# Gram blocks masked over all 128 rows, and a join's correction as one masked addition

## The chip, the core and the metric

One core of a Trainium2 chip runs the whole program. The metric is device microseconds of one execution, from the first instruction to the last.

## What is computed

The program chains three things. First a delta-rule recurrence over 768 tokens for 4 batches and 8 heads of 48 columns, then a gated product, then a soft mixture of experts:

```python
k_n = k / (norm(k) + 1e-6)
for t in range(S):                       # per batch and head, state is 48 x 48
    y[t]  = q[t] @ state
    v_old = state.T @ k_n[t]
    state = state + beta[t] * outer(k_n[t], v[t] - v_old)
x = (x @ w1) * (x @ w2) @ w3 @ w_out     # 3072 tokens, 384 -> 1024 -> 1024 -> 384
logits = x @ phi                         # 32 slots
dispatch = softmax(logits, over tokens); combine = softmax(logits, over slots)
out = combine @ experts(dispatch.T @ x)
```

Inputs arrive in float32 and, for some weights, float64.

## The kernel before, in words

The recurrence runs in 24 steps of 32 tokens. For each step the 32 x 32 Gram blocks of the keys (one for each batch and head) are multiplied on TensorE (PE), masked to their lower triangle by VectorE (DVE), and the inverse of a unit lower triangular matrix is formed from them. Four steps make a solve: 128 blocks, one to a lane. Steps are taken in pairs, and a pair's keys and queries lie in one tile of seven "slots" of 512 columns. Rows 64 to 112 hold batches 0 and 1 (slots 3 to 6), rows 0 to 48 batches 2 and 3 (slots 3 to 0): in the lower half the order of what is needed runs downwards. So in the products' result (tile `gp`, `g` or `p`) the Gram block is the first block of a head for two batches and the last one for the other two, and the scores and the products across the two steps also lie at different places in the two halves of the rows.

`g_step` issues those products (L420), `g_evac` brings them out of PSUM: the Gram blocks by one masked multiplication for rows 0 to 63 and one for rows 64 to 127 (L369, into tile `dg`); the scores through a copy on ScalarE (ACT, L380) and a masked multiplication on GpSimd (POOL) or DVE (L389, L396); the products across steps by ACT (L402). A PSUM bank is given to the next user when all of these have read it.

The first two solves use halves: `sub16` inverts the two 16 x 16 diagonal blocks on DVE, `join` puts them together and turns them (L523, L525), and `join2(n4)`, one for each of the four steps, forms the block below the diagonal by two sets of 32 x 2 small products on PE (L534, then L541 from the tile `xn`, 16 columns a block) with a copy on ACT between them (L538). Its result, 16 rows in each of the four groups of 32 rows, is subtracted from `w` by four DVE operations of 16 rows (L545). The later four solves take all 32 rows at once on DVE (L501, L504).

Beside the recurrence run the conversions of the float64 weights (L284 to L301 for the gates' weights, tiles `t_w`, `gx`, `raw_w`; then tile `hold` for w_out and w3, with products on PE, L316 to L350, that yield the logits' weights `wphi`), and the gated products of each pair of steps, "a chunk" (L687, tile `ab`, 144 matmuls in eight groups a chunk, 12 chunks). Steps are listed with a time each; a scheduler turns the list into one order per engine, and each engine runs its own order strictly, waiting at semaphores. The tile `ab` and the Gram products of steps 4 to 7 share two PSUM banks.

Of the kernel before, what the change touches and what calls it, by code (L numbers as in the profile page):

```python
# [21 lines left out]
C = 32  # tokens of one step of the recurrence  # L22
NST = S // C
NCH = NST // 2  # two steps: 256 rows of the products that follow
NSS = NST // 4  # four steps: 128 blocks of 32 x 32, one to a lane
NE = 8

# columns of the constant block
# [8 lines left out]
C_N = 418  # L37
# [56 lines left out]
def make_consts():  # L94
    c = np.zeros((128, C_N), np.float32)
    p = np.arange(128)
    i = np.arange(32)
    c[:, C_ID:C_ID + 128] = np.eye(128)
    c[p, C_ID4 + p % 32] = 1.0
    c[:, C_REP:C_REP + 128] = (p[:, None] % 32) == (p[None, :] % 32)  # L100
    c[:, C_ML:C_ML + 32] = i[None, :] <= (p[:, None] % 32)
    # a row's own batch's columns, of two; from C_MA on the other's
    for h in range(3):
        c[:, C_MU + 32 * h:C_MU + 32 * h + 32] = (i[None, :] > (p[:, None] % 32)) & ((p[:, None] // 32) % 2 == h % 2)
    c[:, C_QM] = (p // 32) % 2 == 0
    c[:, C_EB] = -(896.0 + 20.0) * 2.0**23
    return c


def diag(ap):  # L110
    """of each row of NE groups of 36, the first 4 of each: expert e's columns among its 32 from 32e on"""
    return ap[:, :, :].rearrange("p f (e s) -> p f e s", s=36)[:, :, :, 0:4]
# [3 lines left out]
def kern(ctx, tc, kq, vt, kt, bl, w12, w3, wo, phi, w1e, w2e, consts, out):  # L116
# [38 lines left out]
    ecT = pc.tile([128, NSS, 128], F32, name="ecT")  # L155
    u4 = pc.tile([128, 512], F32, name="u4")
# [3 lines left out]
    # two of four copies, for high and for low parts  # L160
# [5 lines left out]
    # the gates' weights, high and low parts, a column block of both in one tile  # L166
    wsl = [pv.tile([128, 2, 2, 3, 128], F32R, name=f"wsl{f}") for f in range(8)]
    # v of a step (rows of its batch) and the state (the other half's rows), batch by batch
    sv = px.tile([128, 4, H * D], F32, name="sv")
    sacc = [ps.tile([128, 512], F32, name=f"sacc{i}") for i in range(2)]  # L170
    # two steps at a time; keys and queries by column of their products: what is multiplied with the state in the rows of
    # the state, the scores in the others. Of the slots 3 has the first step's keys of all batches; 4 its queries, 5 and 6
    # the second step's keys and queries of the first two batches; 2, 1 and 0 likewise of the last two.
    kls = [pw.tile([128, 7, 512], F32, name=f"kl{i}") for i in range(3)]

    # the other weights' conversion takes turns in it, then the converted w_out comes back to it
# [4 lines left out]
    def warm(n, after):  # L181
        """keeps the array's clock up while it waits for what follows"""
# [4 lines left out]
    # once those weights are converted, pairs of steps take turns in it too  # L187
    held4 = hold[:, 0:7 * 512].rearrange("p (k c) -> p k c", k=7)

    def kl_of(p):  # L190
        """where the keys and queries of a pair of steps are"""
# [3 lines left out]
    def before(p):  # L195
        """the pair of steps that was there before"""
# [8 lines left out]
    def when(t, *steps, label="when"):  # L205
        """steps at time t, in the order given"""
# [13 lines left out]
    def srow(b):  # L220
        """rows of the state of batch b"""
# [5 lines left out]
    def trow(n, b):  # L227
        """rows of the tokens of a step: the first step of two has the batches of a pair the other way round"""
# [47 lines left out]
    def to_f32(r, n, name):  # L276
# [6 lines left out]
        # sign * 2^(e - 20)  # L283
# [3 lines left out]
        # the mantissa, 2^20 .. 2^21  # L287
# [38 lines left out]
    def w3_steps():  # L326
        part = {}

        def cv(f, j0):
            """row block f, column blocks j0 .."""  # L330
# [25 lines left out]
    Dg = {}  # L356

    def own(r, c):
        """of a half's columns those of batch c of the two"""
        return r.rearrange("p (h c i) -> p h c i", h=H, c=2)[:, :, c]  # L360

    def g_evac(n, hs, gp, at_, via):
        """gp: row, head, block, column; at_: which block the Gram block, the scores and the two across steps are"""
        s, n4 = divmod(n, 4)
        t, nh = kl_of(n // 2), len(hs)
        if "g" in at_:
            for i in range(2):
                r = slice(64 * i, 64 * i + 64)
                V.tensor_tensor(out=Dg[s][r, 8 * n4 + hs[0]:8 * n4 + hs[0] + nh, :], in0=gp[r, :, at_["g"][i], :],  # L369
                                in1=cs[r, C_ML:C_ML + 32].unsqueeze(1).to_broadcast([64, nh, 32]), op=ALU.mult)  # L370
# [3 lines left out]
        src = [gp[64 * i:64 * i + 64, :, at_["p"][i], :] for i in range(2)]  # L374
# [8 lines left out]
        for i in range(2):  # L383
            r = slice(64 * i, 64 * i + 64)
            if n % 2 == 0:
                # each batch's in its own columns, zeros in the other's
# [5 lines left out]
            for c in range(2):  # L392
# [6 lines left out]
                else:  # L399
                    x = at_["x"][i]  # L400
                    to = t[ro, (5, 0)[i]:(5, 0)[i] + 2, cols].rearrange("p k (h c i) -> p k h c i", h=nh, c=2)
                    A.copy(to[:, :, :, 1 - c], gp[ro, :, x:x + 2, :].rearrange("p h k i -> p k h i"))  # L402

    def g_step(n, hs, which="gp"):
        """of a step's keys with the keys and queries of it and, from the first of two steps, of the second"""
# [5 lines left out]
        # first and last slot of each half's  # L411
# [5 lines left out]
        for h in hs:  # L417
            for b in range(4):
                r, kc, j = srow(b), kcol(h, b), b // 2
                T.matmul(gp[trow(n, b), h - hs[0]], lhsT=t[r, k[j], kc], rhs=t[r, span[j][0]:span[j][1], kc],  # L420
                         start=True, stop=True)
        blocks = {}
        if "g" in which:
            blocks["g"] = (0, nb - 1)
        if "p" in which:
            o = len(which) - 1
            blocks["p"] = (o, nb - 1 - o)
            blocks["x"] = (o + 1, 0)
        g_evac(n, hs, gp, blocks, n < PP)

    def g_parts(p):
        """of two steps"""
# [7 lines left out]
    def solve_steps(s):  # L440
# [4 lines left out]
        def a():  # L445
# [8 lines left out]
            # 1/sqrt: a first guess from the exponent, then Newton steps  # L454
# [30 lines left out]
            if halves:  # L485
                st["tmp"] = sm[:, 5:9].rearrange("p a b -> p (a b)")
                st["xf"] = pk.tile([128, 32, 32], F32, tag="L", name=f"xf{s}", bufs=NL)
                xn = (u4[:, :], ecT[:, 0:4, :].rearrange("p s c -> p (s c)"))[s]
                st["xn"] = xn.rearrange("p (u c) -> p u c", c=16)
# [4 lines left out]
        def sub(j):  # L494
            # two column ranges in turn: neither waits for its own result
# [11 lines left out]
        def sub16(j):  # L507
            # the two diagonal blocks in turn
# [8 lines left out]
        def join():  # L517
            """the block below the diagonal ones: minus the product of the lower one, the Gram block and the upper one"""
# [8 lines left out]
        def join2(n4):  # L527
# [11 lines left out]
            for u in range(8):  # L539
                for b in range(4):  # L540
                    T.matmul(p2[32 * b:32 * b + 16, u], lhsT=xn[qrow(b), 8 * n4 + u, :], rhs=t1[qrow(b), u, :],  # L541
                             start=True, stop=True, tile_position=(32 * b, 32 * b))
            for b in range(4):
                r = slice(32 * b, 32 * b + 16)
                V.tensor_tensor(out=w[r, us, 16:32], in0=w[r, us, 16:32], in1=p2[r], op=ALU.subtract)  # L545
# [14 lines left out]
    xT = {}  # L560

    def copy(n, b, o, i):
        """two engines at the start, when nothing hides the recurrence"""
# [5 lines left out]
    def chain_steps(n):  # L569
# [13 lines left out]
        def ks():  # L583
            # the second step takes the first's part along
# [59 lines left out]
    def join_max():  # L644
        """running maxima of the token streams joined; how much of each stream's sums is left"""
# [19 lines left out]
    ecs, early_g = {}, []  # L665

    def main_steps(c):
# [56 lines left out]
        def soft():  # L724
# [29 lines left out]
            # weights of the slots for each token  # L754
# [13 lines left out]
        def uu():  # L768
# [12 lines left out]
            else:  # L781
                # the last ones with what is left of each stream
# [27 lines left out]
    def behind0(f):  # L810
        """VectorE's part of f after the first inverses"""
# [5 lines left out]
    def behind_w12(f, k):  # L817
        """VectorE's part of f after that of the k-th conversion"""
# [5 lines left out]
    def close_att():  # L824
        """the attention's memory goes to the first weights that follow"""
# [440 lines left out]
```

## Time and profile before

| | before |
|---|---|
| runs | 664.26 us median of 3 (664.17 to 665.92) |
| span of the profiled execution | 663.6 us |
| PE busy | 566.2 us, 85% |
| DVE busy | 425.8 us, 64% |
| ACT busy | 279.8 us, 42% |
| POOL busy | 160.6 us, 24% |
| mean granted clock of TensorE | 0.882 of full speed |

PE is the busiest engine over the whole span, but not in every stage. The first 41 us are keys, Gram blocks and the first solve; up to about 215 us weights are converted; up to about 612 us the recurrence and the gated products fill PE; the rest is the experts. A stage's limit is read from its own rows: the table of windows tells which engine is nearly always busy, the chain of waits tells what was last.

### The profile page before, as it was taken

What the parts mean: (1) busy time and instruction counts of PE and PEld (TensorE: products, weight loads), DVE (VectorE), ACT (ScalarE), POOL (GpSimd) and SP (SyncE); (2) the same over time, 40 slices, a digit from 0 to 9 for tenths busy, and PEclk for the clock granted to TensorE, in tenths of its full rate; (3) what the DMA queues carried; (4) which work ended last, traced back from release to release, by engine and by line L of the source; (5) the groups of instructions that cost most, each with busy time, mean ns of one, the idle gap of its engine ahead of it and who ended that gap; (6) DMA issues with size and microseconds to landing.
All of it is one profiled execution on the core that took longest, in us unless ns stands there. A gap on an engine that the chain in (4) does not pass through costs nothing.

```text
span 663.6 us, 26054 instructions
## 1 busy us (share of the span) xinstructions
PE 566.2 (85%) x11417; PEld 470.5 (71%) x11417; DVE 425.8 (64%) x1315; ACT 279.8 (42%) x704; POOL 160.6 (24%) x213
## 2 busy tenths in 40 slices
PE   5345635888999799899988998998999999999996
PEld 4234534786778677677878886887878899885464
DVE  4997899999887136984379833997993313133214
ACT  1516552435555256444444354444434444333113
POOL 1725865423452026122030101103110000000100
PEclk7555658877979799899999897999999999999997
DMA  9903503448653720400404013030445040678848
GB/s 199 321 9 126 166 0 124 146 122 214 211 158 116 171 67 17 124 2 15 106 4 93 2 34 86 15 82 14 117 125 183 31 147 3 240 253 283 338 182 277
DMA packets 36945, 81.72 MB, mean 123 GB/s; under 512 B 4352, under 2 KB 17792, under 8 KB 35584
## 3 DMA queue, kind: packets, MB, share of 16 engines
q1 hardware_dynamic: 36832, 80.07, 40.1%
q8 instruction: 89, 1.46, 0.9%
q14 instruction: 24, 0.20, 0.1%
HBM read 69.57 MB, written 10.49 MB: 121 GB/s over the span
## 4 chain that ended last, share of the span: by engine, by line
PE 48%; DVE 35%; issue 5%; DMA 5%; POOL 3%; ACT 2%; SPq 0%; DVEq 0%; POOLq 0%; ACTq 0%
PE ab L687 22%; DVE tmp L501 4%; DVE xl L504 4%; PE gp L704 2%; PE gp L420 2%; PE yp L612 2%; DMA kl<-kq 2%; PE ks L591 2%; PE sacc L1111 2%; DVE dg L369 2%; PE hp L1090 2%; DVE xl L481 2%; PE vp L602 2%; PE sacc L622 2%; DVE gl L448 1%
## 5 line engine op out<-in xcount | busy, mean ns | idle before, releaser
L687 PE MATMUL ab<-xT,wsl 128*128 128x256 f32 x1728 | 258.3, 302 | 8.5 <-issue 3.3
L687 PEld LDWEIGHTS ab<-xT,wsl 128*128 128x128 f32 x1728 | 229.3, 202 | 23.3 <-issue 10.0
L696 DVE TENSOR_TENSOR gT<-ab,bs 128x256 f32<-128x256 f32 x84 | 35.0, 419 | 93.6 <-ACT bs L691 78.0
L691 ACT COPY bs<-ab 128x256 f32<-128x256 f32 x96 | 35.7, 372 | 83.3 <-PE ab L687 82.0
L577 POOL TENSOR_TENSOR v<-v,nnT 128x384 f32<-128x384 f32 x24 | 21.6, 900 | 137.0 <-DMA v<-vt 52.1
L504 DVE TENSOR_TENSOR xl<-xl,tmp 128x84 f32<-128x84 f32 (+35 forms) x220 | 50.2, 259 | 0.8
L567 ACT COPY sv<-vp 32x384 f32<-32x384 f32 x96 | 45.1, 470 | 13.1 <-PE vp L602 11.2
L501 DVE TENSOR_TENSOR tmp<-xl 128x84 f32<-128x84 f32 (+35 forms) x220 | 49.8, 259 | 0.6
L420 PE MATMUL gp<-kl 48*32 48x64 f32 (+1 forms) x1024 | 37.8, 280 | 13.0 <-ACT kl L402 8.7
L293 POOL TENSOR_TENSOR hold<-hold 128x384 f32<-128x384 f32 (+1 forms) x32 | 34.2, 1070 | 54.6 <-DVE hold L290 19.3
L420 PEld LDWEIGHTS gp<-kl 48*32 48x32 f32 x1024 | 26.8, 122 | 19.2 <-ACT kl L402 8.8
L705 ACT COPY gtok<-gp 128x512 f32<-128x512 f32 x48 | 28.1, 587 | 18.8 <-PE gp L704 14.9
L612 PE MATMUL yp<-sv,kl 112*32 112x48 f32 (+2 forms) x1280 | 28.4, 220 | 3.8 <-ACT sv L567 3.8
L389 POOL TENSOR_TENSOR kl<-praw,cs 64x256 f32<-64x256 f32 x28 | 22.6, 808 | 36.0 <-ACT praw L380 34.6
L402 ACT COPY kl<-gp 32x256 f32<-32x256 f32 x64 | 23.2, 363 | 19.2 <-DVE kl L389 13.1
L612 PEld LDWEIGHTS yp<-sv,kl 112*32 112x32 f32 (+2 forms) x1280 | 21.9, 118 | 10.0 <-POOL kl L389 4.1
L704 PE MATMUL gp<-cs,gT 128*128 128x128 f32 x168 | 27.5, 281 | 1.5 <-DVE xT L638 1.3
L602 PE MATMUL vp<-v,w 32*32 32x48 f32 x1536 | 26.1, 211 | 2.1 <-DVE w L552 1.4
L602 PEld LDWEIGHTS vp<-v,w 32*32 32x32 f32 x1536 | 21.1, 110 | 8.6 <-issue 3.5
L369 DVE TENSOR_TENSOR dg<-gp,cs 64x128 f32<-64x128 f32 (+1 forms) x60 | 19.8, 330 | 11.4 <-PE gp L420 10.6
L285 ACT ACTIVATE hold<-hold,cs 128x384 int32<-128x384 int32 (+1 forms) x32 | 18.7, 589 | 19.6 <-DVE hold L284 19.1
L396 POOL TENSOR_TENSOR kl<-praw,cs 32x256 f32<-32x256 f32 x28 | 23.4, 835 | 13.7 <-ACT praw L380 12.1
(250 smaller groups left out, 997.9 us busy)
## 6 DMA issues: line engine op xcount, KB each, us to landing
hold<-w SPq DMA_DIRECT2D x16, 384.0 KB, 3.7
v<-vt SPq DMA_DIRECT2D x24, 192.0 KB, 3.0
kk<-kt SPq DMA_DIRECT2D x12, 384.0 KB, 6.6
unitg<-w1e SPq DMA_DIRECT2D x6, 768.0 KB, 5.3
kl<-kq SPq DMA_DIRECT2D x8, 512.0 KB, 7.1
kl<-kq SPq DMA_DIRECT2D x8, 384.0 KB, 5.0
gx<-w SPq DMA_DIRECT2D x4, 768.0 KB, 8.1
raw_w<-w SPq DMA_DIRECT2D x4, 768.0 KB, 8.8
```

Source lines behind the costliest of these rows:

```text
L293: G.tensor_tensor(out=w, in0=m, in1=w, op=ALU.mult)
L369: V.tensor_tensor(out=Dg[s][r, 8 * n4 + hs[0]:8 * n4 + hs[0] + nh, :], in0=gp[r, :, at_["g"][i], :], in1=cs[r, C_ML:C_ML + 32].unsqueeze(1 ...
L420: T.matmul(gp[trow(n, b), h - hs[0]], lhsT=t[r, k[j], kc], rhs=t[r, span[j][0]:span[j][1], kc], start=True, stop=True)
L501: V.tensor_tensor(out=tmp[:, 0:n, lo:hi], in0=x[:, j + 1:32, j:j + 1].to_broadcast([128, n, hi - lo]), in1=x[:, j:j + 1, lo:hi].to_broadca ...
L504: V.tensor_tensor(out=x[:, j + 1:32, lo:hi], in0=x[:, j + 1:32, lo:hi], in1=tmp[:, 0:n, lo:hi], op=ALU.add)
L567: A.copy(o, i)
L602: T.matmul(p[o, h * D:(h + 1) * D], lhsT=w[o, 8 * n4 + h, :], rhs=r[o, h, :], start=True, stop=True, tile_position=(o.start, o.start))
L612: T.matmul(p[qrow(b), h * D:(h + 1) * D], lhsT=kl[r, (6, 0)[b // 2] if t2 else (4, 2)[b // 2], kcol(h, b)], rhs=sv[r, b, h * D:(h + 1) * D ...
L687: T.matmul(o, lhsT=w[:, m, k], rhs=x[:, k], start=(n == 0), stop=(n == 8))
L691: A.copy(bs, p[:, 256:512])
L696: V.tensor_tensor(out=gt, in0=p[:, 0:256], in1=bs, op=ALU.mult)
L704: T.transpose(p[:, t * 256 + i * 128:t * 256 + (i + 1) * 128], gt[:, t * 128:(t + 1) * 128], ident)
```

## The change

In the products of the half with batches 2 and 3 the slots are read backwards (a step of -1 over the slots in the moving operand). The blocks of all four batches then lie in the same order: the Gram block first, then the scores, then the products across steps. The Gram mask becomes one DVE operation over 128 rows instead of two over 64; ACT's copy of the two products across steps reads the lower half's two blocks in reverse. In a join the second product takes 32 columns of `xn` at a time (16 of the block, 16 of the next one) and so writes all 32 rows of a group; a constant column that is -1 in the first 16 rows of each 32 and 0 in the others multiplies the result, and one operation over 128 rows adds it to `w`. For the last block's 16 columns beyond the end, `u4` and `ecT` become parts of one tile `sums`, and GpSimd clears 16 columns behind each `xn`. Comments are dropped, which the diff here leaves out; lines below L420 lie 4 further on.

```diff
+C_LO = 418
-C_N = 418
+C_N = 419
+    c[:, C_LO] = -1.0 * (p % 32 < 16)

-    ecT = pc.tile([128, NSS, 128], F32, name="ecT")
-    u4 = pc.tile([128, 512], F32, name="u4")
+    sums = pc.tile([128, 512 + NSS * 128], F32, name="sums")
+    u4, ecT = sums[:, 0:512], sums[:, 512:512 + NSS * 128].rearrange("p (s c) -> p s c", c=128)

         if "g" in at_:
-            for i in range(2):
-                r = slice(64 * i, 64 * i + 64)
-                V.tensor_tensor(out=Dg[s][r, 8 * n4 + hs[0]:8 * n4 + hs[0] + nh, :], in0=gp[r, :, at_["g"][i], :],
-                                in1=cs[r, C_ML:C_ML + 32].unsqueeze(1).to_broadcast([64, nh, 32]), op=ALU.mult)
+            V.tensor_tensor(out=Dg[s][:, 8 * n4 + hs[0]:8 * n4 + hs[0] + nh, :], in0=gp[:, :, at_["g"], :],
+                            in1=cs[:, C_ML:C_ML + 32].unsqueeze(1).to_broadcast([128, nh, 32]), op=ALU.mult)
...
-                    A.copy(to[:, :, :, 1 - c], gp[ro, :, x:x + 2, :].rearrange("p h k i -> p k h i"))
+                    src_x = gp[ro, :, x:x + 2, :] if i == 0 else gp[ro, :, x + 1:x - 1:-1, :]
+                    A.copy(to[:, :, :, 1 - c], src_x.rearrange("p h k i -> p k h i"))
...
-                T.matmul(gp[trow(n, b), h - hs[0]], lhsT=t[r, k[j], kc], rhs=t[r, span[j][0]:span[j][1], kc],
-                         start=True, stop=True)
+                lo, hi = span[j]
+                slots = slice(lo, hi) if j == 0 else slice(hi - 1, lo - 1 if lo else None, -1)
+                T.matmul(gp[trow(n, b), h - hs[0]], lhsT=t[r, k[j], kc], rhs=t[r, slots, kc], start=True, stop=True)
...
-                xn = (u4[:, :], ecT[:, 0:4, :].rearrange("p s c -> p (s c)"))[s]
-                st["xn"] = xn.rearrange("p (u c) -> p u c", c=16)
+                st["xnf"] = xn = (sums[:, 0:528], sums[:, 544:1072])[s]
+                if s < 2:
+                    G.memset(xn[:, 512:528], 0.0)
+                st["xn"] = xn[:, 0:512].rearrange("p (u c) -> p u c", c=16)
...
-                    T.matmul(p2[32 * b:32 * b + 16, u], lhsT=xn[qrow(b), 8 * n4 + u, :], rhs=t1[qrow(b), u, :],
-                             start=True, stop=True, tile_position=(32 * b, 32 * b))
-            for b in range(4):
-                r = slice(32 * b, 32 * b + 16)
-                V.tensor_tensor(out=w[r, us, 16:32], in0=w[r, us, 16:32], in1=p2[r], op=ALU.subtract)
+                    T.matmul(p2[qrow(b), u], lhsT=st["xnf"][qrow(b), 16 * (8 * n4 + u):16 * (8 * n4 + u) + 32],
+                             rhs=t1[qrow(b), u, :], start=True, stop=True, tile_position=(32 * b, 32 * b))
+            V.scalar_tensor_tensor(out=w[:, us, 16:32], in0=p2, scalar=cs[:, C_LO:C_LO + 1], in1=w[:, us, 16:32],
+                                   op0=ALU.mult, op1=ALU.add)
```

The scheduler also orders what is around these operations anew. On DVE, between the last gates' weights (`t_w7`) and the first conversions in `hold`, the masks of steps 6 and 7 (`gp6`, `gp7`, into `dg1`) stood like this before:

```order
L369 TENSOR_TENSOR dg1_953<-gp6_0_1131,cs_90 64x128 x2
L286 SCALAR_TENSOR_TENSOR t_w7_751<-gx_72,t_w7_751 128x768
L288 TENSOR_SCALAR gx_72<-gx_72 128x768
L369 TENSOR_TENSOR dg1_953<-gp6_4_1159,cs_90 64x128 x2
L290 SCALAR_TENSOR_TENSOR gx_72<-gx_72 128x768
L284 TENSOR_SCALAR hold_115<-hold_115 128x384 x4
L286 SCALAR_TENSOR_TENSOR hold_115<-hold_115 128x384 x2
L288 TENSOR_SCALAR hold_115<-hold_115 128x384
L286 SCALAR_TENSOR_TENSOR hold_115<-hold_115 128x384
L288 TENSOR_SCALAR hold_115<-hold_115 128x384
L369 TENSOR_TENSOR dg1_953<-gp7_0_1187,cs_90 64x256 x2
```

and stand like this in the changed kernel (its L286, L288, L290, L292 are the L284, L286, L288, L290 of before):

```order
L288 SCALAR_TENSOR_TENSOR t_w7_744<-gx_72,t_w7_744 128x768
L642 TENSOR_TENSOR xT0_1_862<-xp1_1110,xT0_0_861 128x3x128
L290 TENSOR_SCALAR gx_72<-gx_72 128x768
L292 SCALAR_TENSOR_TENSOR gx_72<-gx_72 128x768
L286 TENSOR_SCALAR hold_114<-hold_114 128x384 x4
L288 SCALAR_TENSOR_TENSOR hold_114<-hold_114 128x384 x2
L290 TENSOR_SCALAR hold_114<-hold_114 128x384
L369 TENSOR_TENSOR dg1_943<-gp6_0_1118,cs_90 128x128
L288 SCALAR_TENSOR_TENSOR hold_114<-hold_114 128x384
L290 TENSOR_SCALAR hold_114<-hold_114 128x384
L292 SCALAR_TENSOR_TENSOR hold_114<-hold_114 128x384
```

The first mask of step 6 moved behind ten conversion operations and one other; the second one moved behind fourteen conversion operations, that of step 7 (after the rows shown) behind eight.

On PE, where step 7's products and the first gated products (`ab0_0`) begin, before:

```order
L420 MATMUL gp6_0_1131<-kl0_112 32x128 x14
L420 MATMUL gp6_4_1159<-kl0_112 32x128 x14
L534 MATMUL j00_2_1440<-w0_559,dg0_147 32x16 x7
L420 MATMUL gp7_0_1187<-kl0_112 32x64 x32
L687 MATMUL ab0_0_1342<-xT0_0_871,wsl0_101 128x256
L687 MATMUL ab0_0_1342<-xT0_1_872,wsl0_101 128x256
```

and in the changed kernel (L318 is the L316 of before, a turn of converted w_out):

```order
L424 MATMUL gp6_0_1118<-kl0_111 32x128 x14
L424 MATMUL gp6_4_1145<-kl0_111 32x128 x14
L538 MATMUL j00_2_1425<-w0_555,dg0_146 32x16 x7
L424 MATMUL gp7_0_1172<-kl0_111 32x64 x32
L318 MATMUL wot0_1316<-cs_90,hold_114 128x128 x3
L691 MATMUL ab0_0_1327<-xT0_0_861,wsl0_100 128x256
L691 MATMUL ab0_0_1327<-xT0_1_862,wsl0_100 128x256
```

The turn of the first converted w_out block now stands ahead of the first gated product. At the end of the conversions, the last product for `wphi` (L350, tile `w3tw376`) stood behind 272 gated products (L687) in PE's order and stands behind 241 now.

## Rows read from the trace of the kernel before

**Rows 1.** The page: busy time, share of the span and instructions of each engine
```profile
PE 566.2 (85%) x11417; PEld 470.5 (71%) x11417; DVE 425.8 (64%) x1315; ACT 279.8 (42%) x704; POOL 160.6 (24%) x213
```

**Rows 2.** Windows: stretch, its length, busy of PE, PEld, DVE, ACT, POOL; clock, DMA
```profile
41.00:105.00 64.00, 35.69 (x989) 30.22 (x990) 55.38 (x73) 33.29 (x68) 38.16 (x27) 0.55 0.26 78
105.00:160.00 55.00, 45.07 (x899) 39.12 (x900) 52.22 (x163) 22.09 (x50) 21.54 (x20) 0.76 0.52 156
160.00:215.00 55.00, 51.54 (x980) 41.89 (x968) 46.61 (x111) 29.42 (x74) 25.59 (x27) 0.94 0.59 172
...
400.00:500.00 100.00, 91.76 (x1941) 78.99 (x1940) 83.96 (x326) 40.12 (x103) 16.79 (x41) 0.97 0.27 72
```

**Rows 3.** Chain that ended last, 0 to 41 us: start, us, what
```profile
14.48 0.41 DVE dg L369
...
14.91 0.44 DVE dg L369
```

**Rows 4.** The same chain, 37 to 215 us: masks, a join's subtractions, a conversion on POOL
```profile
46.61 0.28 DVE w L545
...
49.14 1.85 POOL t_w L293
...
74.07 0.33 DVE dg L369
74.41 0.43 DVE dg L369
...
200.72 0.29 DVE w L545
```

**Rows 5.** Groups by form: line engine op, tiles, shapes xcount | busy us, mean ns | idle before
```profile
L420 PE MATMUL gp<-kl 48*32 48x128 f32 x512 | 25.9, 318 | 4.3 <-DMA kl<-kq 3.8 <-issue 0.5
...
L369 DVE TENSOR_TENSOR dg<-gp,cs 64x128 f32<-64x128 f32 x40 | 11.5, 287 | 9.6 <-PE gp L420 8.9
...
L534 PE MATMUL j<-w,dg 32*32 32x16 f32 x512 | 9.8, 200 | 13.4 <-DVE w L525 10.6 <-DVE w L545 2.9
L545 DVE TENSOR_TENSOR w<-w,j 16x128 f32<-16x128 f32 x32 | 9.8, 305 | 1.4 <-PE j L541 0.9
...
L534 PEld LDWEIGHTS j<-w,dg 32*32 32x32 f32 x512 | 8.1, 131 | 16.8 <-DVE w L525 10.7 <-issue 6.1
...
L541 PE MATMUL j<-t,u 32*16 32x16 f32 x256 | 3.0, 182 | 4.0 <-ACT t L538 4.0
...
L541 PEld LDWEIGHTS j<-t,u 32*16 32x16 f32 x256 | 2.5, 96 | 5.1 <-ACT t L538 4.6 <-issue 0.6
```

**Rows 6.** Timeline of DVE, 44 to 103 us: start, length (of a run: all), operation
```profile
44.38 0.55 DVE L288 TENSOR_SCALAR gx<-gx 128x768 int32<-128x768 int32 x1
44.85 0.56 DVE L288 TENSOR_SCALAR raw_w<-raw_w 128x768 int32<-128x768 int32 x1
...
89.99 0.58 DVE L369 TENSOR_TENSOR dg<-gp,cs 64x128 f32<-64x128 f32 x2
...
94.20 0.59 DVE L369 TENSOR_TENSOR dg<-gp,cs 64x128 f32<-64x128 f32 x2
94.82 0.96 DVE L290 SCALAR_TENSOR_TENSOR gx<-gx 128x768 f32<-128x768 uint32 x1
95.70 4.44 DVE L284 TENSOR_SCALAR hold<-hold 128x384 int32<-128x384 int32 x4
```

**Rows 7.** Timeline of PE, 93 to 107 us; in brackets the idle time before and its releaser
```profile
93.83 1.93 PE L420 MATMUL gp<-kl 48*32 48x64 f32 x64 [8.73 <-ACT kl L402]
...
96.99 3.98 PE L687 MATMUL ab<-xT,wsl 128*128 128x256 f32 x18 [1.23 <-ACT kl L402]
...
103.89 2.88 PE L687 MATMUL ab<-xT,wsl 128*128 128x256 f32 x12 [2.93 <-ACT praw L380]
```

**Rows 8.** What PE waited for, 400 to 500 us: us in total, times, longest
```profile
PE gp L420 <- DMA kl<-kq: 3.8, 3, 1.7
...
PE vp L602 <- DVE w L552: 1.4, 1, 1.4
```

More of the change, by code (lines that the diff above doesn't have):

```diff
@@ L373, in g_evac @@
         cols = slice(64 * hs[0], 64 * hs[0] + 64 * nh)
-        src = [gp[64 * i:64 * i + 64, :, at_["p"][i], :] for i in range(2)]
+        src = [gp[64 * i:64 * i + 64, :, at_["p"], :] for i in range(2)]
         E = V
@@ L399, in g_evac @@
                 else:
-                    x = at_["x"][i]
+                    x = at_["x"]
                     to = t[ro, (5, 0)[i]:(5, 0)[i] + 2, cols].rearrange("p k (h c i) -> p k h c i", h=nh, c=2)
-                    A.copy(to[:, :, :, 1 - c], gp[ro, :, x:x + 2, :].rearrange("p h k i -> p k h i"))
+                    src_x = gp[ro, :, x:x + 2, :] if i == 0 else gp[ro, :, x + 1:x - 1:-1, :]
+                    A.copy(to[:, :, :, 1 - c], src_x.rearrange("p h k i -> p k h i"))
     def g_step(n, hs, which="gp"):
@@ L419, in g_step @@
                 r, kc, j = srow(b), kcol(h, b), b // 2
-                T.matmul(gp[trow(n, b), h - hs[0]], lhsT=t[r, k[j], kc], rhs=t[r, span[j][0]:span[j][1], kc],
-                         start=True, stop=True)
+                lo, hi = span[j]
+                slots = slice(lo, hi) if j == 0 else slice(hi - 1, lo - 1 if lo else None, -1)
+                T.matmul(gp[trow(n, b), h - hs[0]], lhsT=t[r, k[j], kc], rhs=t[r, slots, kc], start=True, stop=True)
         blocks = {}
         if "g" in which:
-            blocks["g"] = (0, nb - 1)
+            blocks["g"] = 0
         if "p" in which:
-            o = len(which) - 1
-            blocks["p"] = (o, nb - 1 - o)
-            blocks["x"] = (o + 1, 0)
+            blocks["p"] = o = len(which) - 1
+            blocks["x"] = o + 1
         g_evac(n, hs, gp, blocks, n < PP)
```

## The prediction

> **What bounds the kernel now.** I read the busy times first. PE works 85% of the span and DVE 64% [rows 1], and by that line alone a change that only relieves DVE would be worth nothing. So I went on to the windows, stage by stage [rows 2]. From 41 to 105 us DVE is busy 55.4 of 64.0 us and PE 35.7; from 105 to 160 us DVE 52.2 of 55.0 and PE 45.1. There DVE is the limit: PE stands still 28.3 + 9.9 = 38.2 us in these two stages, most of it behind conversions. From 160 to 215 us both are near full (PE 51.5, DVE 46.6 of 55.0), and later PE is the limit (91.8 of 100.0 between 400 and 500 us), although DVE has 84.0 of work there. Third came the chain that ended last. It shows whether the operations touched here were ever what the end waited for: they were. The last two of the eight opening masks stand in it [rows 3], and so do ten subtractions of joins and nine masks between 41 and 215 us, of which the first and the last subtraction and the pair at 74 us are shown [rows 4]. POOL has a part in this chain as well: a conversion's 1.85 us on it [rows 4], so in the first stage not all is DVE.
>
> **What is removed from DVE.** A mask's time follows its elements per row: 287 ns for 64 rows of 128 elements, 305 ns for a subtraction with 16 rows of 128 elements [rows 5]. A quarter of the rows made nothing cheaper, so I take 128 rows at the price of 64, and the masked addition, with 128 elements a row again, at 0.30 us. It reads one operand more than a subtraction; its ends are 0.27 (no dearer than the shortest pieces) and 0.60 us (twice a subtraction), which would be 8 x 0.30 = 2.4 us back.
>
> Counted on the chain: of the opening pair one operation goes, 0.44 us [rows 3]. Of the masks from 41 to 215 us one of each pair goes; the pair at 74 us gives 0.43 [rows 4], that at 94 us 0.30, at 102 us 0.43 (a 256-element mask like the one at 74 us), at 180 us 0.29, at 183 us 0.34, together 1.8. Of the four subtractions of a join three go: the chain has three at 46, 113 and 126 us and one at 200 us, ten by 0.29 [rows 4], 2.9 us. The sum is 0.4 + 1.8 + 2.9 = **5.1 us**. The ends are 0 (what is not DVE in the chain takes over) and all that DVE saves before 215 us whether on the chain or not, nine mask pairs (six by 0.29, three by 0.43), six joins by 0.87, and the opening 0.44, 8.7 us.
>
> A second, smaller gain follows from the order on DVE. Two ordinary operations overlap: the one at 44.38 us lasts 0.55 and the next begins at 44.85, 0.08 us before its end. Behind a pair of masks this is not so: the pair from 94.20 us lasts 0.59, and the next operation begins at 94.82, 0.03 us after its end [rows 6]. With one start row for all, the follower may overlap again: 0.11 us for each of the ten runs counted above, 1.1 us, or nothing where the follower waits anyway. I take 0.5.
>
> After 215 us the chain still holds twelve masks' pairs, one of each worth 0.29 to 0.44 us, 4.4 us in all by the sizes above. But PE is nearly always busy there, and of its waits between 400 and 500 us only one, 1.4 us for a solve's end on DVE, is behind this work, while the longest is for a load of keys [rows 8]. I take 0.4 us, with ends 0 and 4.4.
>
> **What is added.** The second product of a join loads 32 columns of weights where it loaded 16. The first product, which has 32 columns already, keeps PE 9.8 us for 512 records, the second 3.0 us for 256 [rows 5]: 1.2 against 0.75 us a join, so at most 8 x 0.47 = 3.8 us. Later joins lie beside other work of PE; only the first has nothing but the recurrence's start behind it. I take 0.5, ends 0 and 3.8. The weight loads themselves took 96 ns with 16 columns and 131 ns with 32 [rows 5]. The Trainium skill (TensorE: Matmul & The Clock Gate, section on LDWEIGHTS, loading the stationary operand) says that a load's time goes with the number of columns alone, so it would double; the trace shows 1.4 times. By the skill's rule the eight joins' loads would go from 2 x 2.5 to 10.0 us, and all of it on the path would eat the gain.
>
> GpSimd's two clears of 16 columns and the longer row of constants I cost at nothing: GpSimd is idle three quarters of the span [rows 1] and they stand at the start, before it has scores to mask. Were that cover gone, two of its shortest operations would be late by themselves. The merged tile brings no new wait that I can find in the order; the operations on it wait for the same engines as before.
>
> **What is moved.** The masks of steps 6 and 7 stand later in DVE's order. Who waits for them is on PE: step 7's products began at 93.83 us after 8.73 us behind ACT's copies, the first gated products at 96.99 us, the next at 103.89 us after 2.93 behind ACT's copy of the scores [rows 7], and these copies come behind the masks at 89.99 and 94.20 us [rows 6]. The first mask now has the four conversions of 4.44 us [rows 6] and six others ahead of it, the second six more. With the time saved before it (about 2.5 us), I put the first gated products some 7 us later. Those at 96.99 us are 3.98 us of PE's work [rows 7], done in a gap before and now to be done later; PE has 9.9 us of idleness in the next stage [rows 2] in which they fit, if DVE lets it. I charge a third, 1.3 us, ends 0 and 4.0.
>
> **The sum.** -5.1 - 0.5 - 0.4 + 0.5 + 1.3 = -4.2 us. The profiled execution's span is 663.6 us, the median of the runs 664.3; what lies around the span is 0.7 us and doesn't change. From the span 659.4, from the median **660.1 us**.
>
> **Rivals.** *The gain is handed to PE and ends there.* At the end of the conversions PE's order has 241 gated products behind it instead of 272 (the change's section). One costs 258.3 us of busy time by 1728 in the trace, 0.15 us, so PE has 31 x 0.15 = 4.6 us more left to do at that moment. If the conversions end earlier by the 5.1 us and PE is the limit from there on, the end moves by 0.5 us: 663.8 us, no change. For it speaks PE's 51.5 of 55.0 us from 160 to 215 us [rows 2]; against it, that what PE has not done before could fill the 9.9 us in which it stood before 160 us.
>
> *Slower, by the late masks.* If the gated products' lag is not made up between 105 and 160 us, because PE's order has turns of converted weights in between that still wait for DVE and POOL, PE carries 4.0 us over into the stages where it is full, against some 1 us of gain left there: 667.3 us. It decides from the point where more than the sum's other terms, 5.5 us, would be lost, or where the conversions do not end earlier: then the lag alone remains.
>
> *Slower, by reading backwards.* No product of the trace steps backwards. The Gram products with 128 columns keep PE 25.9 us [rows 5], half of them with the backward step now. If that made them half as dear again, 13.0 x 0.5 = 6.5 us would come on a full PE: 664.3 - 4.2 + 6.5 = 666.6 us. From a third (4.2 of 13.0) on it eats the gain. Nothing in the trace speaks for it: the moving operand was already read as separate pieces of 32 columns.
>
> *It does not do what it says.* The order has 34 masks for 68 and 8 additions for 32, so DVE's operations go; only a far dearer masked addition could undo it (2.4 us above), and that leaves the result between the first two cases.
>
> **How the numbers follow.** About 0.3%, 2.0 us, is what a measurement of this kernel can tell from no change: faster is below 662.3, slower above 666.3 us. My forecast, DVE's time reaching the end less the lag, has 0.53; its own range is 656.5 to 662.3. No change, PE's share, 0.26. Slower by the late masks 0.16, by backward reading 0.05. So 0.53, 0.26 and 0.21. The lower end is all of DVE's saving before 215 us, 664.3 - 8.7 = 655.6, the upper end the late masks' 667.3 us.
>
> **What the changed profile would show.** DVE's busy time should fall by 34 masks and 24 subtractions: 20 x 0.29 + 14 x 0.43 + 24 x 0.30 = 19 us, from 425.8 to about 407 us [rows 1]. Masks should stay at 287 ns and the additions at 0.27 to 0.33 us. The first solve should begin 0.4 us earlier. Between 41 and 160 us DVE should remain above 85% busy with the conversions ending some 5 us earlier; PE's idleness before 215 us should shrink by about 4 us, or, in the first rival, stay. The first gated products should begin near 104 us. The Gram products' mean, 318 ns for 128 columns [rows 5], should not move. I would be wrong if the conversions are led by POOL or ACT, if the masked addition costs far more than a subtraction, or if the new order opens a gap on PE somewhere that neither order nor chain of before shows.

## The result, and the profile after

The changed kernel takes **657.64 us** (median of 4 runs, 655.6 to 659.15) against 665.09 us (664.17 to 666.9) for the kernel before beside it: a ratio of 0.9875, interval 0.9832 to 0.9919. In a second comparison (below) the ratio was 0.9902, interval 0.9871 to 0.9933. So it is faster by 6.5 to 8.3 us, where 4.2 us were forecast. The page of the changed kernel, and its windows as in [rows 2]:

```profile
PE 565.9 (86%) x11417; PEld 470.4 (72%) x11417; DVE 406.8 (62%) x1257; ACT 279.3 (42%) x704; POOL 167.7 (26%) x215
```

```profile
41.00:105.00 64.00, 35.53 (x992) 30.38 (x990) 54.77 (x67) 33.94 (x69) 44.49 (x29) 0.81 0.32 96
105.00:160.00 55.00, 44.42 (x874) 37.92 (x872) 50.76 (x162) 21.91 (x49) 24.41 (x22) 0.84 0.51 155
160.00:215.00 55.00, 52.60 (x927) 41.56 (x929) 39.67 (x91) 27.98 (x70) 22.14 (x23) 0.85 0.59 176
...
400.00:500.00 100.00, 95.16 (x2041) 81.67 (x2040) 80.31 (x322) 42.80 (x110) 17.73 (x42) 0.98 0.25 71
```

DVE lost 19.0 us of busy time [rows 1], the 19 us that were forecast. PE did no less. From 41 to 215 us it is busy as before: 132.55 of 174.00 us, where [rows 2] adds up to 132.30. Only later is it busier, 95.16 against 91.76 us between 400 and 500 us. (The first clock figure can't be set against [rows 2]: this profile has no clock record in its first 77 us, and the view shows 1.00 there. A second profile of the same kernel shows 0.56 in the first window.)

The groups that answer to [rows 5]: the products with 128 columns, then masks, both products of a join with their weight loads, and the masked addition.

```profile
L424 PE MATMUL gp<-kl 48*32 48x128 f32 x512 | 25.3, 317 | 5.3 <-DMA kl<-kq 4.7 <-ACT kl L404 0.7
...
L369 DVE TENSOR_TENSOR dg<-gp,cs 128x128 f32<-128x128 f32 x20 | 5.7, 286 | 15.3 <-PE gp L424 15.0
L369 DVE TENSOR_TENSOR dg<-gp,cs 128x256 f32<-128x256 f32 x10 | 4.1, 412 | 1.0 <-PE gp L424 1.0
...
L538 PE MATMUL j<-w,dg 32*32 32x16 f32 x512 | 8.7, 198 | 12.1 <-DVE w L529 12.1
L546 PE MATMUL j<-t,sums 32*32 32x16 f32 x512 | 7.7, 192 | 5.5 <-ACT t L542 5.5
...
L546 PEld LDWEIGHTS j<-t,sums 32*32 32x32 f32 x512 | 6.5, 122 | 8.0 <-ACT t L542 6.1 <-issue 1.5 <-ACT bs L695 0.2
...
L548 DVE SCALAR_TENSOR_TENSOR w<-j,cs,w 128x128 f32<-128x128 f32 x8 | 2.7, 339 | 4.5 <-PE j L546 4.5
```

A mask over 128 rows costs what one over 64 rows did (286 against 287 ns), the masked addition 339 ns where 300 were taken, and the products with 128 columns, half of them read backwards now, 317 against 318 ns on the mean. But an operation's length isn't what the next one pays. DVE's timeline (start, length, operation) of the changed kernel:

```profile
45.75 0.95 DVE L292 SCALAR_TENSOR_TENSOR raw_w<-raw_w 128x768 f32<-128x768 uint32 x1
46.62 0.35 DVE L548 SCALAR_TENSOR_TENSOR w<-j,cs,w 128x128 f32<-128x128 f32 x1
46.88 0.28 DVE L369 TENSOR_TENSOR dg<-gp,cs 128x128 f32<-128x128 f32 x1
...
94.46 0.28 DVE L369 TENSOR_TENSOR dg<-gp,cs 128x128 f32<-128x128 f32 x1
94.66 0.54 DVE L288 SCALAR_TENSOR_TENSOR hold<-hold 128x384 int32<-128x384 int32 x1
```

and of the kernel before, at its first join:

```profile
46.30 1.23 DVE L545 TENSOR_TENSOR w<-w,j 16x128 f32<-16x128 f32 x4
47.57 1.50 DVE L290 SCALAR_TENSOR_TENSOR raw_w<-raw_w 128x768 f32<-128x768 uint32 x1
```

Both new operations overlap what stands behind them here. From its start to the next start a mask takes 0.20 us (94.46 to 94.66) where a pair took 0.62 (94.20 to 94.82, [rows 6]); a join's addition takes 0.26 us (46.62 to 46.88) where four subtractions took 1.27 (46.30 to 47.57). Where the next operation waits for something else there is nothing to overlap: in this profile the next operation starts before the end of 24 of the 34 masks and of five of the eight additions.

On PE the late masks of steps 6 and 7 show as foreseen, at half the size: step 7's products and the first gated ones, as in [rows 7].

```profile
96.88 1.93 PE L424 MATMUL gp<-kl 48*32 48x64 f32 x64 [8.45 <-ACT kl L404]
99.88 0.90 PE L318 MATMUL wot<-cs,hold 128*128 128x128 f32 x3 [1.07 <-POOL hold L295]
100.43 4.76 PE L691 MATMUL ab<-xT,wsl 128*128 128x256 f32 x23
```

The gated products begin 3.4 us later than in [rows 7], where 7 us were forecast. DVE's conversions of `hold` begin at 88.92 us, 6.8 us earlier than in [rows 6], and the last of them ends at 205.29 us, where it ended at 211.76 us before.

### The profile page after: what moved, and what is told of

Same layout as the page of the kernel before. It is cut to its first block, busy times and chain, and to the rows that moved or that the text cites. A ratio compares the mean times of both kernels' runs of the same rounds, so it can differ in the third digit from the quotient of the medians.

```text
span 657.4 us, 25995 instructions
## 1 busy us (share of the span) xinstructions
PE 565.9 (86%) x11417; PEld 470.4 (72%) x11417; DVE 406.8 (62%) x1257; ACT 279.3 (42%) x704; POOL 167.7 (26%) x215
## 4 chain that ended last, share of the span: by engine, by line
PE 56%; DVE 26%; DMA 6%; issue 5%; POOL 3%; ACT 2%; SPq 0%; DVEq 0%; POOLq 0%; ACTq 0%
PE ab L691 25%; PE gp L424 3%; DMA kl<-kq 3%; DVE tmp L505 3%; PE gp L708 3%; DVE xl L508 2%; PE yp L616 2%; PE ks L595 2%; PE sacc L626 2%; PE sacc L1115 2%; PE vp L606 2%; PE hp L1094 2%; DVE hold L286 2%; PE lp L715 2%; DVE xl L483 1%
## 5 line engine op out<-in xcount | busy, mean ns | idle before, releaser
L295 POOL TENSOR_TENSOR hold<-hold 128x384 f32<-128x384 f32 (+1 forms) x32 | 36.7, 1153 | 50.1 <-DVE hold L292 12.9
L389 POOL TENSOR_TENSOR kl<-praw,cs 64x256 f32<-64x256 f32 x28 | 25.0, 894 | 37.3 <-ACT praw L380 36.0
L287 ACT ACTIVATE hold<-hold,cs 128x384 int32<-128x384 int32 (+1 forms) x32 | 18.7, 590 | 26.8 <-DVE hold L286 26.4
L626 PE MATMUL sacc<-sv,kk 64*48 64x48 f32 x704 | 26.4, 220 | 0.3 <-issue 0.3
```

The costliest lines, as they stand in the source:

```text
L295: G.tensor_tensor(out=w, in0=m, in1=w, op=ALU.mult)
L626: T.matmul(sacc[b % 2][srow(b), h * D:(h + 1) * D], lhsT=k[r, b % 2, h, :], rhs=sv[r, b, h * D:(h + 1) * D], start=False, stop=(c == NCH - 2),
```

## The experiments

Twelve kernels were run, in three sets of four, each set against the kernel before on one chip in five rounds. A difference from the kernel before goes by the ratio (1% is 6.65 us; the intervals reach 1.6 to 3.5 us to either side), one between two kernels of the same set by their medians where nothing else is said.

**The masks alone, the join alone, and the two halves without their saving on DVE.** The first takes the backward reading and the one mask, with the old join; the second only the join.

```diff
 e1_masks_only:  slots read backwards; one mask over 128 rows; four subtractions as before
 e2_join_only:   masks as before; 32 columns in the second product; one masked addition
```

> The slots are read backwards and the Gram masks are one operation over 128 rows; the joins stay as before (16-column second product, four subtractions). The masks of steps 6 and 7 stand where they stood before, ahead of the conversions. Theory 1 (the time that DVE saves before the weights are converted reaches the end): a pair of masks that took 0.62 us from its start to the next operation's start now takes 0.20, so 0.44 + 6 x 0.42 + 3 x 0.55 = 4.6 of the 10.6 us of DVE time that the whole change saves before 215 us; at the whole change's ratio (7.4 us of 10.6) -3.2 us. Theory 2 (the gain is the new order, conversions ahead of the masks of steps 6 and 7): -1 to 0 us. Theory 3 (backward reading costs something, hidden so far): DVE's saving less that cost.

Measured: 658.85 us, ratio 0.9932 (0.9909 to 0.9956), 4.5 us faster.

> Forward reading and two masks of 64 rows as before; the joins as in the change (32-column second product, one masked addition). The scheduler puts the masks of step 6 behind seven to ten conversion operations more, as in the change. Theory 1: six joins before 215 us save 1.0 us each on DVE, 6.0 of 10.6 us, so -4.2 us. Theory 2: nearly the whole, -6 to -7.4 us.

Measured: 662.21 us, ratio 0.9960 (0.9927 to 0.9992), 2.7 us faster. Both parts gain, and together they make up the 6.5 to 8.3 us. Theory 2, by which the masks alone would bring 1 us at most and the join's order the rest, fits neither. Theory 1's 3.2 and 4.2 us lie within the two intervals.

The other two kernels keep what each part puts on PE and give DVE all its operations back:

```diff
 e3_back_two_masks (slots read backwards)
+                V.tensor_tensor(out=Dg[s][r, ...], in0=gp[r, :, at_["g"], :], ...)   # r: two halves of 64 rows
 e4_wide_product (32 columns in the second product)
+            for b in range(4):
+                V.tensor_tensor(out=w[r, us, 16:32], in0=w[r, us, 16:32], in1=p2[r], op=ALU.subtract)
```

> Backward reading, with two masks of 64 rows and the joins as before; the order of DVE and PE is that of before. Theories 1 and 2: 0 us, within 0.3%. Theory 3: slower by what the backward step costs; a Gram product with 128 columns would take more than 318 ns on the mean.

Measured: 666.53 us, ratio 1.0030 (0.9997 to 1.0062): not told from no change.

> The second product of a join with 32 columns and the merged tile, but four subtractions of 16 rows as before, two masks and forward reading. The masks of step 6 stand behind the conversions as in the change, and DVE saves nothing. Theory 1: +0.5 to +2 us (0.3 us more in each second product, the masks late). Theory 2: the order alone gives most of the gain, -4 to -6 us.

Measured: 667.10 us, ratio 1.0035 (1.0008 to 1.0062), 2.3 us slower (0.5 to 4.1). Theory 2 falls: the order without DVE's saving gains nothing. The masks stand late in this kernel as in the changed one (its first gated product begins at 100.55 us), so the 2.3 us are the price of the wide product and of the late masks together. The two groups that matter, of the kernel with backward reading and of the one with the wide product:

```profile
L424 PE MATMUL gp<-kl 48*32 48x128 f32 x512 | 26.2, 320 | 5.8 <-DMA kl<-kq 4.0 <-issue 1.7
```

```profile
L545 PE MATMUL j<-t,sums 32*32 32x16 f32 x512 | 7.5, 193 | 5.3 <-ACT t L542 5.3
```

With half of them read backwards the products take 320 ns on the mean where 318 were taken before; half as much again for the backward ones would have made it 398. So the gain is DVE's: one mask for two is worth the difference of the first kernel and the third, 1.0030 - 0.9932 = 1.0%, 6.5 us; one addition for four that of the second and the fourth, 1.0035 - 0.9960 = 0.75%, 5.0 us. With the two runs' intervals taken together, either figure is good to some 2.8 us.

**Four kernels next to the changed one.** The second comparison of the changed kernel itself:

> The changed kernel itself again, on the chip and in the rounds of the three that follow, so that they can be set against it. Both theories: as measured, 657.6 us against 665.1, a ratio of 0.9875.

Measured: 659.71 us, 0.9902 (0.9871 to 0.9933).

```diff
 h2_early_masks
-G2 = -0.03
+G2 = -0.08
```

> The changed kernel with one number of the table of times moved (G2 from -0.03 to -0.08), so that the masks of steps 6 and 7 stand earlier in DVE's order again: 35, 40 and 51 conversions' operations are ahead of the three instead of 43, 49 and 53 (33, 35 and 45 before the change), and 265 gated products instead of 241 ahead of the last converted w_phi. Theory 1 (DVE's saving gives the gain, and the late masks give some of it back: 1.3 us in the forecast, up to the 2.3 us that the wide second product and the order cost together): 1.3 to 2.3 us less than the changed kernel, a ratio to the kernel before of 0.984 to 0.9855, and a first gated product some 3 us earlier than its 100.4 us. Theory 3 (the late masks cost nothing, since the gated products fit in later gaps; the wide second product is what costs): the changed kernel's time within 0.3%, a ratio of 0.986 to 0.989. Theory 2 (the new order is itself a part of the gain): 1 to 3 us more than the changed kernel, 0.989 to 0.992.

Measured: 660.39 us, 0.9936 (0.9907 to 0.9966). This kernel alters its computation: the products of steps 6 and 7 stand ahead of the load of their keys and queries, and take what lay in that memory. The load now waits 15.6 us for these products, which is a new wait, and is issued at 93.06 us where the changed kernel has it at 75.41 us. So the run doesn't price the late masks, and the forecast's 1.3 us for them stays untested by themselves.

```diff
 h3_one_score_copy
-            for i in range(2):
-                A.copy(raw[64 * i:64 * i + 64], src[i])
+            A.copy(raw, gp[:, :, at_["p"], :])
```

> The changed kernel with ACT's two 64-row copies of a pair's scores made one 128-row copy as well, which the new order of the columns allows: 24 copies fewer on ACT, 16 x 0.26 + 8 x 0.37 = 7 us of its 279. ACT's mean busy share is 42%, and these copies follow the masks. If such a copy's second half is what POOL's products of keys and scores wait for (36.0 us of POOL's idleness ends with these copies), up to 0.3 us for each of the 12 pairs before 215 us, 3 us, comes back: a ratio of 0.983. If POOL and ACT have room, as their shares say: the changed kernel's time, 0.986 to 0.989. I lean to the second.

Measured: 657.76 us, 0.9897 (0.9845 to 0.9948), the changed kernel's ratio. 24 operations fewer on ACT, which is 43% busy, bring nothing that can be told; with this interval a gain of some 3 us isn't excluded either.

```diff
 h4_late_pairs
-            V.tensor_tensor(out=Dg[s][:, ...], in0=gp[:, :, at_["g"], :], ...)
+            for r in (slice(0, 128),) if s < 2 else (slice(0, 64), slice(64, 128)):
+                V.tensor_tensor(out=Dg[s][r, ...], in0=gp[r, :, at_["g"], :], ...)
```

> The changed kernel with the masks of steps 8 to 31 in two operations of 64 rows again, and one of 128 rows for steps 0 to 7 alone: 24 operations more on DVE, 16 x 0.29 + 8 x 0.42 = 8 us of its time, nearly all after 180 us, where PE has the least idleness. The forecast put the masks after 215 us at 0.4 us with ends 0 and 4.4, and two pairs at 180 us at 0.6. Theory 1 (the gain comes from the stages in which DVE is the limit, before 180 us): 0.4 to 1.0 us more than the changed kernel, a ratio of 0.988 to 0.989. Theory 4 (DVE's time counts later too, since step follows step through its masks and joins): 3 to 5 us more, 0.992 to 0.995.

(The kernel has 24 steps, so these are steps 8 to 23.) Measured: 664.03 us, 0.9980 (0.9945 to 1.0015), **4.3 us more** than the changed kernel beside it, which leads the kernel before by 5.7 us in the same medians. By the ratios the difference is 5.2 us, good to some 3 us. Theory 1, which was the forecast's and allowed 1.0 us, falls: the masks of steps 8 to 23, from 178 us on, hold a large part of the gain, by these medians more than half.

**Where a mask's time counts.** Each mask of one stage is made four operations, and the last kernel changes the order alone.

```diff
 i1_first_masks_4x (s < 2), i2_masks_8_15_4x (s in (2, 3)), i3_masks_16_23_4x (s > 3)
+            for r in (slice(0, 64), slice(64, 128)) * 2 if s < 2 else (slice(0, 128),):
 i4_other_order
-GA = (0.2, 0.06)
+GA = (0.22, 0.08)
```

> The changed kernel with each of the ten masks of steps 0 to 7 (before 105 us) made four operations: two of 64 rows, and the same two again, which write the same values. That is 3 x (6 x 0.43 + 4 x 0.29) = 11 us more on DVE, in the stages in which DVE stands least; all else is as in the changed kernel. Theory A (DVE's time counts by the stage: nearly all of it before 215 us, as the forecast had it): 8 to 11 us more than the changed kernel, a ratio to the kernel before of 1.000 to 1.007. Theory B (what is gained or lost before 215 us is mostly handed to PE's later work, the forecast's first rival; the later stages decide): 1 to 4 us more, 0.990 to 0.996.

Measured: 671.01 us, 1.0105 (1.0067 to 1.0143).

> The same for the twelve masks of steps 8 to 15, which stand between 178 and 293 us: 3 x (8 x 0.29 + 4 x 0.42) = 12 us more on DVE. The kernel has 24 steps, so steps 8 to 23 are all that the run with pairs again for later steps changed, by 8 us of DVE for some 4 us of time. Theory A: DVE's time is hidden by PE after 215 us, and that run's loss is its order's: 0 to 2 us more than the changed kernel, a ratio of 0.990 to 0.993. Theory B (between 258 and 300 us the solve of steps 8 to 11 fills DVE while PE waits, so a mask there counts in full): 5 to 10 us more, 0.997 to 1.005.

Measured: 662.02 us, 0.9959 (0.9926 to 0.9991).

> The same for the twelve masks of steps 16 to 23, after 320 us: 12 us more on DVE. Theory A: 0 to 2 us more than the changed kernel, 0.990 to 0.993. Theory B: less than for steps 8 to 15, since PE stands 4.8 of 100 us between 400 and 500 us in the changed kernel; 3 to 8 us, 0.994 to 1.002.

Measured: 671.72 us, 1.0104 (1.0064 to 1.0143).

> The changed kernel with no work added, only another order: two numbers of the table of times moved by 0.02 of a chunk, so that the Gram products and masks of steps 8 to 23 are put a little later. 317 rows of PE's order differ from the changed kernel's and 240 of DVE's, much as in the run with pairs again for later steps (412 and 269). Theory B (DVE's time is what counts): the changed kernel's time within 0.3%, 0.987 to 0.993. Theory C (such orders by themselves are worth several us, and the pairs' loss was one): 3 us or more to either side, outside 0.985 to 0.995.

Measured: 658.17 us, 0.9895 (0.9854 to 0.9935), the changed kernel's ratio. This other order by itself brings nothing, so theory C finds no support. Against this kernel the first masks cost 12.8 us for 11 us of added operations, those of steps 8 to 15 3.9 us for 12, and those of steps 16 to 23 13.6 us for 12; each of these is good to some 4 us. That is neither A nor B: early and latest masks count in full, the middle ones by a third. Why the middle ones count less was not tested. Six of these twelve stand between 236 and 258 us in the changed kernel, and from 215 to 258 us its DVE is busy only 11.92 of 43.00 us, so that operations more may have found room there.

PE shows where the time goes. Windows 41 to 258 and 258 to 500 us (columns as in [rows 2]), of the kernel before, the changed one, and those with late pairs, with four operations in steps 0 to 7, in steps 8 to 15, in steps 16 to 23, and with the other order. (The clock of the first window can't be compared in the changed kernel's profile and in the last, whose first clock records lie 77 to 78 us into the span.)

```profile
41.00:258.00 217.00, 170.53 (x3791) 143.06 (x3792) 168.41 (x388) 105.03 (x244) 97.15 (x99) 0.77 0.44 126
258.00:500.00 242.00, 224.69 (x4758) 194.31 (x4758) 178.72 (x685) 105.09 (x268) 42.47 (x85) 0.96 0.23 58
```

```profile
41.00:258.00 217.00, 170.91 (x3901) 143.25 (x3902) 157.13 (x353) 106.85 (x249) 105.41 (x104) 0.87 0.43 126
258.00:500.00 242.00, 229.90 (x4876) 198.81 (x4864) 174.15 (x673) 106.85 (x273) 42.20 (x81) 0.96 0.24 61
```

```profile
41.00:258.00 217.00, 173.20 (x3792) 145.44 (x3784) 155.91 (x355) 103.92 (x243) 98.97 (x96) 0.77 0.44 126
258.00:500.00 242.00, 223.32 (x4739) 193.69 (x4740) 178.03 (x683) 105.69 (x268) 43.35 (x87) 0.95 0.23 58
```

```profile
41.00:258.00 217.00, 160.91 (x3770) 135.16 (x3774) 162.51 (x370) 105.38 (x244) 101.78 (x103) 0.76 0.44 126
258.00:500.00 242.00, 226.28 (x4746) 196.39 (x4738) 168.68 (x661) 104.35 (x267) 40.69 (x81) 0.96 0.22 56
```

```profile
41.00:258.00 217.00, 168.67 (x3792) 141.83 (x3792) 163.58 (x375) 104.58 (x244) 104.99 (x103) 0.76 0.44 126
258.00:500.00 242.00, 226.89 (x4852) 195.75 (x4853) 178.58 (x686) 107.63 (x274) 40.36 (x81) 0.98 0.24 61
```

```profile
41.00:258.00 217.00, 169.90 (x3858) 142.59 (x3859) 156.81 (x351) 106.24 (x247) 103.57 (x101) 0.78 0.44 126
258.00:500.00 242.00, 219.41 (x4667) 189.27 (x4665) 179.27 (x700) 103.16 (x263) 40.68 (x83) 0.97 0.22 53
```

```profile
41.00:258.00 217.00, 171.37 (x3789) 143.72 (x3790) 156.52 (x350) 103.70 (x241) 100.52 (x91) 0.85 0.43 126
258.00:500.00 242.00, 227.42 (x4976) 196.40 (x4978) 175.03 (x677) 110.33 (x282) 47.33 (x94) 0.99 0.24 61
```

PE's idle time is the window less the first number after it. From 258 to 500 us it is 17.3 us before, 12.1 in the changed kernel, 18.7 with the late pairs back, 15.1 with four operations a mask in steps 8 to 15, and 22.6 with four in steps 16 to 23. What the first masks' operations cost shows from 41 to 258 us: 56.1 us against 46.1. Such sums are no price by themselves. With the other order it is 14.6 us, 2.5 more than in the changed kernel, for the same ratio; and the profile with the late pairs is of that kernel's longest run, 667.88 us. What PE waits for between 350 and 500 us (us in total, times, longest) in the changed kernel, and with four operations in steps 16 to 23:

```profile
PE gp L424 <- DMA kl<-kq: 4.7, 2, 2.4
PE ab L691 <- DVE gT L700: 1.5, 2, 1.1
...
PE ep L794 <- DVE ec L770: 0.3, 1, 0.3
```

```profile
PE gp L426 <- DMA kl<-kq: 3.9, 3, 2.3
PE ab L693 <- DVE soft L737: 3.2, 1, 3.2
PE up L779 <- DVE xT L644: 2.6, 1, 2.6
...
PE ab L693 <- DVE gT L702: 2.3, 1, 2.3
```

The gated products wait there for `soft` and `gT`, DVE's operations behind a solve and its masks. PE works 229.9 of these 242.0 us, 95%, in the changed kernel, and part of what is left are waits for DVE; with more operations on DVE these waits grew.

## Why the prediction was right, and where it was too small

The sign, its reason and the time are borne out: 657.6 us lies in the range and in the likeliest case's own, and in the second comparison the time was 659.7 us. That the sum came so near is in part luck: it put what DVE gives back at 5.1 + 0.5 + 0.4 = 6.0 us and what is added and moved at 0.5 + 1.3 = 1.8, and by the first four kernels both are about twice that, 6.5 + 5.0 = 11.5 and 2.0 + 2.3 = 4.3, of which the 2.0 isn't told from nothing. Step by step:

- **DVE's operations before 215 us, -5.1 us: the mechanism is right, the size perhaps too small.** For the masks of steps 0 to 7 the chain's count gave 0.4 + 0.43 + 0.30 + 0.43 = 1.6 us. Three operations more on each cost 12.8 us, so one is worth 4.3, if the one taken away counts like those put in. But all masks together are worth 6.5 us by the first set and those of steps 8 to 23 hold 4.3 of it by the second, which leaves 2.2 for the first ten. Between 2.2 and 4.3 these runs don't decide. The joins: 5.0 us for eight, where 2.9 were counted in the chain; 2.9 is still within the interval. The count has two weak points. It took only what stood in the chain of one execution, and it took lengths (0.29 us a mask, 0.87 a join) where the starts shown differ by 0.42 and 1.01. The conversions end 6.5 us earlier, where some 5 were forecast.
- **The follower of a mask overlaps again, -0.5 us: the mechanism is right, the size not measured by itself.** It was allowed for ten runs of operations; the changed profile shows it behind 24 masks and five additions.
- **Masks after 215 us, -0.4 us (ends 0 and 4.4): the step that failed.** With the two pairs near 180 us, the forecast had 0.6 + 0.4 = 1.0 us for the masks of steps 8 to 23. They are worth 4.3 us by the run with pairs again. By the last runs it is 13.6 / 3 = 4.5 for steps 16 to 23, all after 320 us, and 3.9 / 3 = 1.3 for steps 8 to 15, of which three masks stand before 190 us. I had looked at one window, 400 to 500 us, and at what PE's waits there were named for [rows 8]; but from 258 to 500 us PE stands 17.3 us, and this fell to 12.1 us.
- **The wide second product, +0.5 us (ends 0 and 3.8), and the late masks, +1.3 us: together about right, apart not priced.** The run with the wide product, the merged tile and the late masks, and no saving on DVE, lost 2.3 us (0.5 to 4.1) where the two terms add up to 1.8. PE's time for second products is 7.7 us, where it was 3.0 [rows 5] and 3.2 us for the two solves. The late masks delay the first gated product by 3.4 us, not 7: the conversions of `hold` begin 6.8 us earlier, where the forecast took about 2.5 us of time saved before this point, and a part of the 6.8 is that masks no longer stand ahead of them. The rival by which this lag makes the kernel slower falls.
- **Rival, handed to PE: half of its sign is there.** PE's idleness from 41 to 215 us did not shrink, as this rival would have it, and yet the gain reached the end. An engine's idle sum in one stage did not tell where a gain goes. How the early saving, which costs PE's time from 41 to 258 us when taken away, is handed on to later stages is not shown by these runs.
- **Rival, backward reading: falls by the trace.** The products take 317 and 320 ns. The 2.0 us (-0.2 to 4.1) of that run aren't told from nothing: its profile is 1.9 us late at the first solve already, whose first product waits for its keys until 6.22 us where it began at 4.88 us before, and still 1.3 us late at the last gated product.

By the first set the parts add up to -6.5 - 5.0 + 2.0 + 2.3 = -7.2 us, within the 6.5 to 8.3 us measured; with 4.3 us each for early and late masks instead of 6.5 for all it would be -9.3. With some 2 us of uncertainty in each both close, which doesn't show that nothing else is in it. No kernel tried is faster than the changed one beyond the noise.

## What to carry over

Count what an operation is worth from its start to the next start, not by its length: where several operations on parts of the rows became one on all rows, the overlaps with both neighbours came back too. A small saving on the second engine is to be looked for in the idle time of the first, over all stages: a PE that was 93% busy from 258 to 500 us still stood 17.3 us, and a large part of the gain lay with the masks of these later stages. Making the same operations more, stage by stage, told in three runs where they count; what one fewer is worth is then an estimate, to be set against a run that takes it away.

## What the runs showed of the hardware

Around the masks of these traces a DVE operation that has nothing else to wait for starts either some 0.08 us before the end of the one ahead or 0.01 to 0.04 us after it, and the difference goes with the rows at which the operations start. The kernel with four operations a mask in steps 0 to 7 shows it side by side. The order has a mask of rows 0 to 63, one of rows 64 to 127 and the same two again, here among conversions on all rows; the first line is the first two:

```profile
95.25 0.60 DVE L371 TENSOR_TENSOR dg<-gp,cs 64x128 f32<-64x128 f32 x2
...
96.36 0.35 DVE L290 TENSOR_SCALAR hold<-hold 128x384 int32<-128x384 int32 x1
96.75 0.28 DVE L371 TENSOR_TENSOR dg<-gp,cs 64x128 f32<-64x128 f32 x1
96.96 0.54 DVE L288 SCALAR_TENSOR_TENSOR hold<-hold 128x384 int32<-128x384 int32 x1
97.53 0.29 DVE L371 TENSOR_TENSOR dg<-gp,cs 64x128 f32<-64x128 f32 x1
97.85 0.36 DVE L290 TENSOR_SCALAR hold<-hold 128x384 int32<-128x384 int32 x1
```

The conversion behind the third mask begins 0.07 us before its end (96.96 against 97.03); both start at row 0. The fourth mask, which starts at row 64, begins 0.03 us after the end of what is ahead of it (97.50), and the conversion behind it 0.03 us after its own (97.82). That is some 0.1 us for each change of the start row. The third mask itself begins 0.04 us after the end of the conversion ahead (96.71), although both start at row 0: the last operation before it that read PSUM, as a mask does, was the second mask, from row 64 on. So it isn't only the operation just ahead that counts. The Trainium skill (VectorE: DVE Perf Modes, section on two Vector instructions with no wait between them) says that an instruction is held until all earlier ones have finished if an input of it starts in another quadrant of 32 rows than that of the last instruction that read the same memory, or its output in another one than the last output into that memory; these four starts agree with it, if the masks are in the order that the program gives them.

Weight loads with 32 columns took 122 ns where those with 16 took 96 [rows 5] and, in the other solve, 89. The Trainium skill (TensorE: Matmul & The Clock Gate, section on LDWEIGHTS) has them in proportion to the columns; this trace doesn't agree, with 1.3 to 1.4 times for twice the columns.
